# Zero products at TensorE's start made 16 bits and 512 columns wide, and an attention, feed-forward and experts kernel given a further order for its loads and first two blocks

## The chip, the cores and the metric

The kernel runs on one core of one Trainium2 chip. TensorE (PE) multiplies matrices into PSUM banks, VectorE (DVE), ScalarE (ACT) and GpSimd (POOL) do the elementwise work, and SyncE (SP) issues nearly all transfers. Each engine works through its own instructions in order and waits for the others by semaphores. The metric is device time in microseconds (us), the median of several executions.

## The reference

Three layers stand behind one another. The input has 2 sequences of 768 tokens with 8 heads of 64 columns, which makes 1536 tokens of 512 columns.

```python
# 1. attention with decay, in blocks of 64 (lam: one number a head)
intra = (q_b @ k_b.T * Dmask) @ v_b
inter = (q_b * lam_pow) @ kv_state
kv_state = lam**64 * kv_state + (k_b * rev_pow).T @ v_b
# 2. feed-forward, 512 -> 2048 -> 512
h = x @ w_in
g = where(h > 0, h, exp(min(h, 0)) - 1)
x = g @ w_out
# 3. one of 8 experts a token (and none where x @ w_skip <= 0)
y = gate * (relu(x @ w1[e]) @ w2[e])
out = x + y
```

The feed-forward weights come as 64-bit numbers and are made into 32-bit ones on the chip.

## The kernel before, in words

The tokens are worked on in chunks of 128 (12 of them, c = 0 to 11) and in blocks of three chunks. A product of 32-bit accuracy is made of three passes over a high and a low part (PASSES), so every weight and every activation is split in two.

**The prelude.** SyncE starts the loads in the order of LOADS: q and v are the two halves of an attention chunk (kq and kv in the traces), f a feed-forward weight. VectorE clears `zrow`, a table of zeros. TensorE then multiplies zeros by zeros (`warm`, L793 to L796, counts in WARM), with the two small products that build the decay tables (L801, L804) in between. Their results are never read. VectorE builds eight rows of the decay mask.

**The first two blocks.** Attention for chunks 0 to 5 and the first feed-forward steps are issued item by item from the table PLAN. An item is a name and its arguments, and the order of the table sets the order on every engine. A single step can only run when its own engine has come to it and its operands are there. The items that are spoken of below:

- MR:h, one mask row (VectorE, L810); LC, the table of powers lp (ScalarE)
- CV:f, B0:f, B1:f, B2:f, the conversion of weight f from 64 bits (ScalarE L161, VectorE L173, L176, L179); HI:f, its high part (ScalarE L184); LO:f and LP:f, its low part (L188, on VectorE and on GpSimd)
- S:c, the scores of chunk c (TensorE L248); M:c,half, their mask (VectorE L258); V:c, scores times values (TensorE L284)
- KD:c, keys times decay (GpSimd L275); KV:c, keys times values (TensorE L445); ST:c, their addition to the state (L468 for chunk 0 on ScalarE, else VectorE L472); DEC:c, the decay of the state (ScalarE L452)
- QD:c and QE:c, queries times powers (L269, on GpSimd and on VectorE); I:c, scaled queries times state (TensorE L284)
- XH:c, XL:c, the high and low part of the attention's result (L428, L432)
- F1:n, first feed-forward product (TensorE L497); R, X, E, GH, GL its activation in five steps on ScalarE and VectorE; F2:n, the second product (TensorE L544)

After the table (some 137 us into the span) loops with fixed orders take over: the rest of the feed-forward, with the attention of the second sequence between, the choice of experts, and the experts.

Of the kernel before, what the change touches and what calls it, by code (L numbers as in the profile page):

```python
# [10 lines left out]
BF16 = mybir.dt.bfloat16  # L11
# [5 lines left out]
P = 128  # L17
# [14 lines left out]
E = 8  # L32
# [2 lines left out]
XW = DM + 2  # L35
BIG = float(1 << 20)
PASSES = ((0, 0), (0, 1), (1, 0))
LOADS = "f0 q0 q1 v0 v1 q2 v2 q3 v3 f1 v4 q4 f2 q5 v5 f3 f4 f5 f6 f7 f8 f9"
PLAN = """
MR:5 MR:2 MR:0 MR:6 CV:0 S:0 MR:1 B0:0 MR:4 MR:7 B1:0 MR:3 KD:0 B2:0 KD:1 M:0,0 M:0,1 S:1 LC:0  # L40
KV:0 QD:1 ST:0 M:1,1 KD:2 HI:0 M:1,0 V:0 LO:0 XH:0 S:2 I:1 KV:1 M:2,1 QD:2 V:1 DEC:1 S:3 XH:1
ST:1 M:2,0 I:2 DEC:2 KV:2 QD:3 M:3,0 CV:1 KD:3 XL:0 V:2 M:3,1 V:3 ST:2 I:3 XL:1 KD:4 XH:2 XL:2
F1:0 B0:1 XH:3 B1:1 XL:3 B2:1 DEC:3 S:4 CV:2 M:4,1 KV:3 M:4,0 ST:3 R:0 HI:1 QD:4 X:0 E:0 S:5 V:4
I:4 M:5,0 M:5,1 LP:1 KV:4 GH:0 DEC:4 CV:3 GL:0 V:5 B0:2 QE:5 B1:2 F2:0 XH:4 ST:4 B2:2 I:5 XH:5
B0:3 XL:5 HI:2 F1:1 XL:4 F1:2 LP:2 R:1 X:1 E:1 GH:1 R:2 B1:3 X:2 GL:1 CV:4 B2:3 F1:3 F2:1 E:2
B0:4 F1:4 HI:3 GH:2 B1:4 GL:2 R:3 LO:3 X:3 R:4 E:3 X:4 F2:2 B2:4 GH:3 E:4 GL:3 F1:5 CV:5 F2:3
B0:5 HI:4 GH:4 LO:4 CV:6 B1:5 GL:4 B0:6 R:5 B2:5 F1:6 X:5 HI:5 R:6 E:5 B1:6 F2:4 X:6 GH:5 LO:5
F1:7 CV:7 E:6 GL:5 F1:8 GH:6 B2:6 R:7 B0:7 F2:5 X:7 E:7 B1:7 HI:6 GH:7 GL:7 GL:6 LO:6 R:8 X:8
CV:8 F2:6 E:8 GH:8 B2:7 B0:8 F1:9 B1:8 HI:7 GL:8 F1:10 F2:7 LO:7 B2:8 R:9 X:9 E:9 CV:9 B0:9 R:10
X:10 E:10 HI:8 F2:8 B1:9 GH:9 LO:8 B2:9 CV:10 B0:10 GL:9 B1:10 GH:10 HI:9 GL:10 F1:11 F1:12 R:11  # L50
LO:9 X:11 R:12 CV:11 E:11 X:12 F2:9 B2:10 B0:11 E:12 GH:11 F1:13 HI:10 GL:11 R:13 B1:11 B2:11
F2:10 GH:12 F2:11 GL:12 LO:10 F2:12 HI:11 CV:12 LO:11 CV:13 X:13 B0:12 B1:12 E:13 B0:13 F1:14
B2:12 F1:15 GH:13 R:14 X:14 E:14 GL:13 B1:13 GH:14 GL:14 F2:13 R:15 HI:12 LO:12 B2:13 X:15 CV:14
E:15 GH:15 B0:14 F1:16 GL:15 F2:14 B1:14 F2:15 R:16 X:16 E:16 HI:13 GH:16 F1:17 LO:13 CV:15
B2:14 GL:16 R:17 X:17 B0:15 HI:14 B1:15 F1:18 F2:16 E:17 GH:17 R:18 B2:15 X:18 GL:17 LO:14 F1:19
R:19 E:18 F2:17 F1:20 HI:15 GH:18 GL:18 X:19 E:19 F2:18 GH:19 R:20 F1:21 X:20 E:20 GH:20 LO:15
GL:19 F2:19 R:21 X:21 E:21 GL:20 F1:22 R:22 F2:20 GH:21 X:22 GL:21
"""


# [1 line left out]
def kernel(  # L62
# [11 lines left out]
    nc = tc.nc  # L74
# [18 lines left out]
    def bank(tag, bufs):  # L93
        return ps.tile([P, 512], F32, tag=tag, name=tag, bufs=bufs)
# [3 lines left out]
    def aux():  # L98
        return bank(aux_tag[0], 3)
# [9 lines left out]
    zrow = const.tile([P, P], F32, name="zrow")  # L109
# [375 lines left out]
    def where(n):  # L485
        return order[n] if n < 2 * NF else divmod(n, NF)
# [257 lines left out]
    if True:  # L744
# [12 lines left out]

        loads = LOADS.split()
        for item in loads[:3]:
# [19 lines left out]
            load(item)  # L779

        J = 2 * NF - TAIL1
        WARM = (4, 1, 5)
        manual = ExitStack()
        manual.enter_context(tc.manual_schedule())
        cv_gen = conv_ops(16)
# [6 lines left out]

        def warm(b, n):  # L793
            for i in range(n):
                nc.tensor.matmul(out=b[:, 0:P], lhsT=zrow[:, 0:P], rhs=zrow[:, 0:P],
                                 start=True, stop=True)  # L796

        idle_bank = bank("y", 3)
        warm(idle_bank, WARM[0])
        lamb, lpb = aux(), aux()  # L800
        nc.tensor.matmul(out=lamb[:, 0:H], lhsT=ones8, rhs=diag8, start=True, stop=True)  # L801
        warm(idle_bank, WARM[1])
        for k in range(4):
            nc.tensor.matmul(out=lpb[:, k * P:(k + 1) * P], lhsT=sel[:, k, :], rhs=powers,  # L804
                             start=True, stop=True)
        warm(idle_bank, WARM[2])
        nc.vector.tensor_copy(out=lam_b, in_=lamb[:, 0:H])

# [162 lines left out]
        for n in range(J, N - TAIL):  # L971
# [5 lines left out]
            b, f = where(n)  # L977
# [61 lines left out]
        for k in range(4):  # L1039
            nc.tensor.matmul(out=xg0[k // 2][:, k * P:(k + 1) * P],  # L1040
                             lhsT=early[:, k * P:(k + 1) * P], rhs=ident,
# [170 lines left out]
    with tc.If(over > 0):  # L1212
# [4 lines left out]
        for c in range(NCH):  # L1217
            nc.gpsimd.indirect_dma_start(
                out=slots[:, :], out_offset=bass.IndirectOffsetOnAxis(ap=idx[:, c:c + 1], axis=0),
                in_=gates[:, c, :], in_offset=None, bounds_check=E * NTOK - 1, oob_is_err=False)  # L1220
        for e in range(E):
# [3 lines left out]
            with tc.For_i(0, ne):  # L1225
                for k in range(8):
# [8 lines left out]
                    out=gt[:, :], out_offset=None, in_=slots[:, :],  # L1235
# [7 lines left out]
                    out=xg[:, :], out_offset=None, in_=out[:, :],  # L1243
# [73 lines left out]
```

## Time and profile before

| what | value |
|---|---|
| time, median of 3 runs | 437.74 us (437.14 to 438.39) |
| time of the profiled execution | 436.92 us |
| its span, first to last instruction | 434.8 us |
| TensorE busy | 97% of the span |
| VectorE busy | 74% of the span |
| GpSimd busy | 18% of the span |

The profiled execution lies 0.82 us under the median, and 2.1 us of it lie outside the span. TensorE's busy share is modelled, so that 97% says that it hardly waits, not that it runs at its peak.

### The profile page before, as it was taken

The numbers are of one execution on the slowest core, as the hardware profiler recorded it, in microseconds if no ns is written. First come the engines' busy times: TensorE is split into PE (matmuls) and PEld (weight loads), VectorE is DVE, ScalarE is ACT, GpSimd is POOL, SyncE is SP. The second block draws the span as 40 slices with busy tenths as digits, with TensorE's granted clock in tenths as the row PEclk, the third lists the DMA queues.
The fourth block names the chain that finished last, engine by engine and source line by source line (L and its number), as shares of the span: only waits on it lengthen the run. The fifth ranks groups of instructions, "written<-read, shape, count | busy, mean of one in ns | idle before, by whom it ended". The sixth has DMA issues, their size and how long they took to land.

```text
span 434.8 us, 8034 instructions
## 1 busy us (share of the span) xinstructions
PE 422.6 (97%) x3086; PEld 371.1 (85%) x3086; DVE 322.1 (74%) x703; ACT 239.0 (55%) x401; POOL 77.8 (18%) x107
## 2 busy tenths in 40 slices
PE   8999999999999999999999999999999999999992
PEld 8889999889998998998788998889897888888881
DVE  6898999998324447865887758776546799999960
ACT  2675787675443334533233445656526689888830
POOL 3853000001200120003141000222004202222211
PEclk9999999999999999999999999999999999999997
DMA  8999703998002131305141255336456899999301
GB/s 303 415 416 419 286 0 106 260 114 200 1 2 75 58 126 63 123 27 192 61 159 38 72 193 194 131 123 186 142 218 233 312 330 366 400 376 365 134 3 36
DMA packets 27649, 78.92 MB, mean 182 GB/s; under 512 B 4282, under 2 KB 8378, under 8 KB 25552
## 3 DMA queue, kind: packets, MB, share of 16 engines
q1 hardware_dynamic: 26000, 75.28, 51.1%
q0 software_dynamic: 1600, 3.03, 1.8%
q8 instruction: 26, 0.43, 0.4%
q14 instruction: 23, 0.19, 0.2%
HBM read 70.02 MB, written 10.51 MB: 185 GB/s over the span
## 4 chain that ended last, share of the span: by engine, by line
PE 82%; DVE 6%; issue 4%; DMA 3%; ACT 2%; POOL 1%; SPq 0%; POOLq 0%; ACTq 0%
PE h L497 29%; PE y L544 21%; PE h L1097 8%; PE aux L544 8%; PE y L1122 6%; PE aux L284 2%; DMA big<-in_wex_dram 1%; PE y L284 1%; DVE wa L139 1%; DMA big<-in_wff_dram 1%; PE aux L1108 1%; PE aux L599 1%; DMA out_dram<-o,ix 1%; PE aux L584 1%; PE aux L1077 1%
## 5 line engine op out<-in xcount | busy, mean ns | idle before, releaser
L497 PE MATMUL h<-xT,wa 128*128 128x384 f32 x480 | 89.8, 337 | 0.0
L497 PEld LDWEIGHTS h<-xT,wa 128*128 128x128 f32 x480 | 83.6, 188 | 3.0 <-issue 0.6
L544 PE MATMUL y<-wa,g 128*128 128x512 f32 x270 | 68.1, 396 | 0.0
L523 ACT ACTIVATE g<-e 128x384 fp32r<-128x384 f32 x64 | 33.5, 523 | 47.9 <-DVE e L517 47.9
L502 ACT ACTIVATE e<-h 128x384 f32<-128x384 f32 x64 | 31.0, 485 | 50.8 <-PE h L497 48.7
L544 PEld LDWEIGHTS y<-wa,g 128*128 128x128 f32 x270 | 49.6, 188 | 9.3 <-DVE g L528 0.3
L497 PE MATMUL h<-xT,wb 128*128 128x384 f32 x288 | 54.2, 336 | 0.0
L517 DVE SCALAR_TENSOR_TENSOR e<-e,h 128x384 f32<-128x384 f32 x64 | 35.1, 549 | 24.2 <-ACT e L505 23.9
L497 PEld LDWEIGHTS h<-xT,wb 128*128 128x128 f32 x288 | 50.5, 188 | 2.5 <-issue 0.5
L528 DVE TENSOR_TENSOR g<-e,g 128x384 fp32r<-128x384 f32 x64 | 36.2, 566 | 12.7 <-ACT g L523 12.7
L544 PE MATMUL y<-wb,g 128*128 128x512 f32 x162 | 40.6, 395 | 0.0
L628 DVE CUSTOM_DVE_ANT_0 zrow<-x,big 128x512 int8<-128x512 f32 x54 | 38.2, 707 | 0.6
L1097 PE MATMUL h<-wa,xgT 128*128 128x512 f32 x144 | 36.0, 397 | 0.1
L544 PEld LDWEIGHTS y<-wb,g 128*128 128x128 f32 x162 | 29.9, 188 | 5.5
L505 ACT ACTIVATE e<-e 128x384 f32<-128x384 f32 x64 | 33.5, 524 | 1.8
L139 DVE TENSOR_TENSOR wa<-big,wa 128x1024 fp32r<-128x1024 f32 x22 | 26.7, 1240 | 7.2 <-ACT wa L138 7.0
L1097 PEld LDWEIGHTS h<-wa,xgT 128*128 128x128 f32 x144 | 26.5, 188 | 5.7 <-ACT xgT L575 0.3
L727 POOL DMA_INDIRECT xe<-x,idx x12 | 12.2, 1015 | 98.2 <-DVE s L700 43.6
L343 POOL TENSOR_TENSOR big<-big,mask 128x512 f32<-128x512 f32 x6 | 7.3, 1214 | 106.6 <-DVE g L528 64.9
L138 ACT ACTIVATE wa<-big 128x1024 fp32r<-128x1024 f32 x22 | 22.4, 1057 | 3.9 <-DMA big<-in_wex_dram 3.9
L1122 PE MATMUL y<-wa,ht 128*128 128x512 f32 x96 | 23.7, 398 | 0.0
L139 DVE TENSOR_TENSOR wa<-ahead,wa 128x1024 fp32r<-128x1024 f32 x18 | 21.7, 1250 | 2.7 <-ACT wa L138 2.5
(231 smaller groups left out, 697.7 us busy)
## 6 DMA issues: line engine op xcount, KB each, us to landing
big<-in_wex_dram SPq DMA_DIRECT2D x17, 1024.0 KB, 6.1
ahead<-in_wex_dram SPq DMA_DIRECT2D x15, 1024.0 KB, 7.0
wb<-in_wff_dram SPq DMA_DIRECT2D x10, 1024.0 KB, 14.6
big<-in_wff_dram SPq DMA_DIRECT2D x6, 1024.0 KB, 8.9
big<-in_wgt_dram SPq DMA_DIRECT2D x18, 256.0 KB, 3.3
big<-in_kq_dram SPq DMA_DIRECT2D x6, 512.0 KB, 4.4
big<-in_kv_dram SPq DMA_DIRECT2D x6, 512.0 KB, 6.3
out_dram<-x SPq DMA_DIRECT2D x12, 256.0 KB, 2.6
```

The costliest lines, as they stand in the source:

```text
L138: nc.scalar.activation(out=w[:, 0, cs], in_=src, func=ACTF.Copy)
L139: nc.vector.tensor_tensor(out=w[:, 1, cs], in0=src, in1=w[:, 0, cs].bitcast(F32), op=ALU.subtract)
L497: nc.tensor.matmul(out=h, lhsT=w[:, wi, k * P:(k + 1) * P], rhs=xT[b][:, xi, k, :], start=(j == 0), stop=(j == 11))
L502: nc.scalar.activation(out=e, in_=h_t[n], func=ACTF.Relu, scale=-1.0)
L505: nc.scalar.activation(out=e_t[n], in_=e_t[n], func=ACTF.Exp, scale=-1.0)
L517: nc.vector.scalar_tensor_tensor(out=e, in0=e, scalar=-1.0, in1=h_t.pop(n), op0=ALU.add, op1=ALU.max)
L523: nc.scalar.activation(out=g[:, 0, :], in_=e, func=ACTF.Copy)
L528: nc.vector.tensor_tensor(out=g[:, 1, :], in0=e_t.pop(n), in1=g[:, 0, :].bitcast(F32), op=ALU.subtract)
L544: nc.tensor.matmul(out=y_t[b, t], lhsT=g[:, gi, t * P:(t + 1) * P], rhs=w[:, wi, 512:1024], start=(f == 0 and i == 0), stop=(f == NF - 1 a ...
L628: nc.vector.tensor_tensor_reduce(out=junk, in0=x2_t[c][:, 0:DM], in1=cols[0][:, slot * DM:(slot + 1) * DM], scale=1.0, scalar=0.0, op0=ALU ...
L1097: nc.tensor.matmul(out=h, lhsT=xgT_t[e][:, xi, k * P:(k + 1) * P], rhs=w_t[NF + 8 * e + k][:, wi, j * 512:(j + 1) * 512], start=(i == 0), ...
L1122: nc.tensor.matmul(out=y, lhsT=ht[:, hi, k, :], rhs=w_t[NF + 8 * e + 4 + k // 2][:, wi, (k % 2) * 512:(k % 2) * 512 + 512], start=(i == 0) ...
```

## The change

Three things change. The zero products read `zrow` as 16-bit numbers, and each fills a whole bank (512 columns in place of 128 columns of 32-bit numbers); their counts go from 4, 1 and 5 to 5, 2 and 5. In LOADS v0 now stands ahead of q1, and q4 ahead of v4. PLAN gets another order; most of it lies in the first two blocks, and further on single items move by a few places. In it QD:1 becomes QE:1 (from GpSimd to VectorE), LP:2 becomes LO:2 (the same way), and LO:14 becomes LP:14 (the other way).

```diff
-LOADS = "f0 q0 q1 v0 v1 q2 v2 q3 v3 f1 v4 q4 f2 q5 v5 f3 f4 f5 f6 f7 f8 f9"
+LOADS = "f0 q0 v0 q1 v1 q2 v2 q3 v3 f1 q4 v4 f2 q5 v5 f3 f4 f5 f6 f7 f8 f9"
 PLAN = """
-MR:5 MR:2 MR:0 MR:6 CV:0 S:0 MR:1 B0:0 MR:4 MR:7 B1:0 MR:3 KD:0 B2:0 KD:1 M:0,0 M:0,1 S:1 LC:0
+MR:2 CV:0 S:0 MR:6 MR:1 MR:0 MR:7 B0:0 MR:5 MR:4 MR:3 B1:0 M:0,0 KD:0 M:0,1 B2:0 S:1 LC:0 M:1,0
...
-        WARM = (4, 1, 5)
+        WARM = (5, 2, 5)
...
         def warm(b, n):
             for i in range(n):
-                nc.tensor.matmul(out=b[:, 0:P], lhsT=zrow[:, 0:P], rhs=zrow[:, 0:P],
+                nc.tensor.matmul(out=b, lhsT=zeros[:, 0:P],
+                                 rhs=zeros.rearrange("p (o n) -> p o n", o=1).to_broadcast([P, 2, 2 * P]),
                                  start=True, stop=True)
 
+        zeros = zrow.bitcast(BF16)
```

On VectorE, from the mask rows to the low part of the first weight, stood before (L810 mask rows, L173, L176 and L179 the bits of weight 0, L258 masks on scores, L188 the low part of weight 0):

```order
L810 SCALAR_TENSOR_TENSOR mask<-tab 128x128 x5
L173 TENSOR_SCALAR v<-v 128x1024
L810 SCALAR_TENSOR_TENSOR mask<-tab 128x128 x2
L176 SCALAR_TENSOR_TENSOR v<-big,v 128x1024
L810 SCALAR_TENSOR_TENSOR mask<-tab 128x128
L179 SCALAR_TENSOR_TENSOR v<-big,v 128x1024
L258 TENSOR_TENSOR pm_store<-h,mask 128x512 x2
L258 TENSOR_TENSOR pm_store<-y,mask 128x512 x2
L188 TENSOR_TENSOR wa<-v,wa 128x1024
```

On the same engine at the same place stands now (the mask rows are L812):

```order
L812 SCALAR_TENSOR_TENSOR mask<-tab 128x128 x5
L173 TENSOR_SCALAR v<-v 128x1024
L812 SCALAR_TENSOR_TENSOR mask<-tab 128x128 x3
L176 SCALAR_TENSOR_TENSOR v<-big,v 128x1024
L258 TENSOR_TENSOR pm_store<-h,mask 128x512 x2
L179 SCALAR_TENSOR_TENSOR v<-big,v 128x1024
L258 TENSOR_TENSOR pm_store<-y,mask 128x512
L269 TENSOR_TENSOR wb<-wb,lp 128x512
L258 TENSOR_TENSOR pm_store<-y,mask 128x512
L188 TENSOR_TENSOR wa<-v,wa 128x1024
```

The last mask row moved ahead of L176, both masks of chunk 0 moved ahead of L179, and the query scaling of chunk 1 (L269) stands between the masks of chunk 1.

On GpSimd the first products stood before as key scaling (L275) of chunks 0 and 1, query scaling (L269) of chunk 1, and so on with chunk 2:

```order
L275 TENSOR_TENSOR wb<-wb,mask 128x512 x2
L269 TENSOR_TENSOR wb<-wb,lp 128x512
L275 TENSOR_TENSOR wb<-wb,mask 128x512
L269 TENSOR_TENSOR wb<-wb,lp 128x512
L269 TENSOR_TENSOR wa<-wa,lp 128x512
```

On GpSimd at the same place stands now:

```order
L275 TENSOR_TENSOR wb<-wb,mask 128x512 x3
L269 TENSOR_TENSOR wb<-wb,lp 128x512
L269 TENSOR_TENSOR wa<-wa,lp 128x512
L275 TENSOR_TENSOR wa<-wa,mask 128x512 x2
L269 TENSOR_TENSOR wa<-wa,lp 128x512
```

The query scaling of chunk 1 is gone from it, so the three key scalings of chunks 0 to 2 follow one another. On TensorE the order of the items of the first two blocks is as before; only the zero products ahead of them differ.

## Rows read from the trace of the kernel before

**Rows 1.** The page: the span.

```profile
span 434.8 us, 8034 instructions
```

**Rows 2.** Busy time by stage; columns PE, PEld, DVE, ACT, POOL, granted clock, DMA.

```profile
12.00:35.00 23.00, 22.18 (x341) 19.73 (x341) 21.25 (x33) 15.24 (x31) 14.20 (x20) 1.00 1.02 415
35.00:137.00 102.00, 102.00 (x523) 92.76 (x519) 79.60 (x106) 64.55 (x104) 8.25 (x8) 1.00 0.56 143
```

**Rows 3.** Timeline of TensorE, the first 36 us: start us, us, instruction, idle before.

```profile
1.13 2.07 PE L795 MATMUL y<-zrow 128*128 128x128 f32 x8 [1.13 <-DVE zrow L761]
...
6.19 2.34 PE L795 MATMUL y<-zrow 128*128 128x128 f32 x10
8.46 1.79 PE L248 MATMUL h<-wb 64*128 64x128 f32 x16
10.09 1.06 PE L248 MATMUL y<-wb 64*128 64x128 f32 x16
12.18 0.69 PE L445 MATMUL aux<-wb 128*64 128x64 f32 x16 [1.03 <-POOL wb L275]
...
14.76 1.09 PE L284 MATMUL y<-wb,state 128*64 128x128 f32 x16
```

**Rows 4.** Timeline of SyncE's transfer issues, 5 to 18 us.

```profile
7.41 0.33 SPq L150 DMA_DIRECT2D big<-in_wff_dram  x1
8.70 0.33 SPq L232 DMA_DIRECT2D wa<-in_kv_dram  x1
...
12.54 0.33 SPq L229 DMA_DIRECT2D wa<-in_kq_dram  x1
```

**Rows 5.** Waits of SyncE, 5 to 18 us: total, times, longest.

```profile
SPq L232 <- DMA wb<-in_kq_dram: 0.9, 1, 0.9
```

**Rows 6.** Timeline of VectorE, 4 to 50 us.

```profile
7.30 0.69 DVE L173 TENSOR_SCALAR v<-v 128x1024 int32<-128x1024 int32 x1 [1.33 <-ACT v L161]
7.91 0.73 DVE L810 TENSOR_TENSOR_SCAN mask<-tab 128x128 f32<-128x128 f32 x2
8.55 1.20 DVE L176 SCALAR_TENSOR_TENSOR v<-big,v 128x1024 int32<-128x1024 int32 x1
...
11.12 1.28 DVE L258 TENSOR_TENSOR pm_store<-h,mask 128x512 f32<-128x512 f32 x2
12.32 1.28 DVE L258 TENSOR_TENSOR pm_store<-y,mask 128x512 f32<-128x512 f32 x2
14.87 1.60 DVE L188 TENSOR_TENSOR wa<-v,wa 128x1024 fp32r<-128x1024 f32 x1 [1.27 <-ACT wa L184]
...
26.17 1.28 DVE L258 TENSOR_TENSOR t<-aux,mask 128x512 f32<-128x512 f32 x2
...
31.41 0.68 DVE L269 TENSOR_TENSOR wa<-wa,lp 128x512 f32<-128x512 f32 x1
...
38.61 0.56 DVE L517 SCALAR_TENSOR_TENSOR e<-e,h 128x384 f32<-128x384 f32 x1 [1.34 <-ACT e L505]
...
45.11 1.22 DVE L188 TENSOR_TENSOR wa<-v,wa 128x1024 fp32r<-128x1024 f32 x1
```

**Rows 7.** Timeline of ScalarE, 12 to 15 us.

```profile
12.97 0.78 ACT L468 ACTIVATE state<-aux 64x256 f32<-64x256 f32 x2 [5.23 <-PE aux L445]
13.78 1.06 ACT L184 ACTIVATE wa<-v 128x1024 fp32r<-128x1024 f32 x1
```

**Rows 8.** Timeline of GpSimd, 9 to 14 us.

```profile
10.17 2.96 POOL L275 TENSOR_TENSOR wb<-wb,mask 128x512 f32<-128x512 f32 x2 [6.87 <-DVE mask L810]
```

**Rows 9.** The chain that ended last, 10 to 44 us: start us, us, what.

```profile
10.17 1.96 POOL wb L275
...
27.51 1.16 PE aux L248 x14
...
35.21 6.44 PE h L497 x36
41.65 2.06 PE y L544 x9
```

More of the change, by code (lines that the diff above doesn't have):

```diff
@@ L37 @@
 PASSES = ((0, 0), (0, 1), (1, 0))
-LOADS = "f0 q0 q1 v0 v1 q2 v2 q3 v3 f1 v4 q4 f2 q5 v5 f3 f4 f5 f6 f7 f8 f9"
+LOADS = "f0 q0 v0 q1 v1 q2 v2 q3 v3 f1 q4 v4 f2 q5 v5 f3 f4 f5 f6 f7 f8 f9"
 PLAN = """
-MR:5 MR:2 MR:0 MR:6 CV:0 S:0 MR:1 B0:0 MR:4 MR:7 B1:0 MR:3 KD:0 B2:0 KD:1 M:0,0 M:0,1 S:1 LC:0
-KV:0 QD:1 ST:0 M:1,1 KD:2 HI:0 M:1,0 V:0 LO:0 XH:0 S:2 I:1 KV:1 M:2,1 QD:2 V:1 DEC:1 S:3 XH:1
-ST:1 M:2,0 I:2 DEC:2 KV:2 QD:3 M:3,0 CV:1 KD:3 XL:0 V:2 M:3,1 V:3 ST:2 I:3 XL:1 KD:4 XH:2 XL:2
-F1:0 B0:1 XH:3 B1:1 XL:3 B2:1 DEC:3 S:4 CV:2 M:4,1 KV:3 M:4,0 ST:3 R:0 HI:1 QD:4 X:0 E:0 S:5 V:4
@@ L44 @@
[L44 to L55, printed above, removed]
@@ L56 @@
-R:19 E:18 F2:17 F1:20 HI:15 GH:18 GL:18 X:19 E:19 F2:18 GH:19 R:20 F1:21 X:20 E:20 GH:20 LO:15
-GL:19 F2:19 R:21 X:21 E:21 GL:20 F1:22 R:22 F2:20 GH:21 X:22 GL:21
+MR:2 CV:0 S:0 MR:6 MR:1 MR:0 MR:7 B0:0 MR:5 MR:4 MR:3 B1:0 M:0,0 KD:0 M:0,1 B2:0 S:1 LC:0 M:1,0
+KV:0 KD:1 QE:1 V:0 ST:0 M:1,1 KD:2 HI:0 LO:0 XH:0 S:2 I:1 KV:1 QD:2 DEC:1 ST:1 V:1 S:3 M:2,1
+M:2,0 XH:1 I:2 DEC:2 KV:2 V:2 QD:3 CV:1 M:3,1 M:3,0 XL:0 V:3 ST:2 I:3 XL:1 XH:2 B0:1 KD:3 XL:2
+B1:1 F1:0 DEC:3 XH:3 XL:3 B2:1 S:4 M:4,1 CV:2 KV:3 M:4,0 ST:3 R:0 B0:2 HI:1 KD:4 X:0 S:5 V:4
@@ new lines @@
+M:5,0 QD:4 I:4 E:0 M:5,1 LP:1 KV:4 GH:0 DEC:4 XH:4 CV:3 GL:0 V:5 B1:2 F2:0 QE:5 ST:4 B0:3 B2:2
+XL:4 I:5 XH:5 HI:2 XL:5 F1:1 R:1 LO:2 F1:2 X:1 R:2 E:1 GH:1 B1:3 X:2 GL:1 CV:4 B2:3 F1:3 F2:1
+E:2 B0:4 F1:4 HI:3 GH:2 B1:4 GL:2 R:3 LO:3 X:3 R:4 E:3 X:4 F2:2 B2:4 GH:3 E:4 CV:5 GL:3 F1:5
+F2:3 B0:5 HI:4 GH:4 LO:4 R:5 CV:6 B1:5 GL:4 B0:6 F1:6 X:5 B2:5 HI:5 E:5 R:6 B1:6 F2:4 X:6 GH:5
+LO:5 F1:7 CV:7 E:6 GL:5 F1:8 GH:6 B2:6 R:7 X:7 B0:7 F2:5 E:7 B1:7 HI:6 GH:7 GL:6 GL:7 LO:6 R:8
+X:8 CV:8 F2:6 E:8 GH:8 B2:7 B0:8 F1:9 B1:8 HI:7 GL:8 F1:10 F2:7 LO:7 B2:8 R:9 X:9 E:9 CV:9 B0:9
@@ new lines @@
+R:10 X:10 E:10 HI:8 F2:8 B1:9 GH:9 LO:8 F1:11 B2:9 CV:10 B0:10 GL:9 HI:9 GH:10 B1:10 GL:10 F1:12
+R:11 LO:9 X:11 E:11 R:12 X:12 F2:9 B2:10 CV:11 B0:11 E:12 GH:11 F1:13 HI:10 GL:11 B1:11 B2:11
+F2:10 GH:12 F2:11 R:13 GL:12 LO:10 F2:12 HI:11 CV:12 LO:11 CV:13 X:13 B0:12 B1:12 E:13 B0:13
+F1:14 B2:12 F1:15 R:14 X:14 E:14 GH:13 GL:13 B1:13 GH:14 GL:14 F2:13 R:15 HI:12 LO:12 B2:13 X:15
+CV:14 E:15 GH:15 B0:14 F1:16 GL:15 F2:14 B1:14 F2:15 R:16 X:16 E:16 HI:13 F1:17 LO:13 CV:15
+B2:14 GH:16 GL:16 R:17 X:17 HI:14 B0:15 B1:15 E:17 F1:18 R:18 B2:15 F2:16 X:18 GH:17 LP:14 GL:17
@@ L58 @@
+F1:19 R:19 E:18 F2:17 F1:20 HI:15 GH:18 GL:18 X:19 E:19 GH:19 R:20 F1:21 F2:18 X:20 E:20 GH:20
+LO:15 GL:19 R:21 GL:20 X:21 F1:22 E:21 GH:21 R:22 F2:19 F2:20 X:22 GL:21
 """
```

## The prediction

> **What bounds the kernel now.** I read the busy time by stage first. From 35 to 137 us TensorE is busy for 102.00 of 102.00 us, and in the stage before, 12 to 35 us, for 22.18 of 23.00 [rows 2]. So from 35 us on TensorE is the bound and nothing in the new order can make it shorter; a new order there can only add waits. What can be won is the time by which the dense part begins earlier. In the chain of waits that part shows as one long piece of TensorE from 35.21 us on [rows 9]. The end of the span (434.8 us [rows 1]) follows the start of that piece one to one, if nothing later gives way.
>
> Next I read who holds TensorE back before 35 us. Its timeline shows three places. The zero products and the two small ones run from 1.13 us, and the scores of chunk 0 (S:0) start at 8.46, right behind the last of them. S:0 is slow: 16 instructions take 1.79 us, and the same 16 for chunk 1 (S:1) take 1.06. Then TensorE stands idle for 1.03 us until GpSimd has scaled the keys of chunk 0 (KD:0), which lets KV:0 start at 12.18 [rows 3]. KD:0 itself had waited until 10.17 for the last mask row [rows 8]. The third place is 0.82 us of idle time between 12 and 35 us [rows 2]; in the chain it lies ahead of S:5, whose last 14 instructions start at 27.51 [rows 9], 0.06 us behind VectorE's masks of chunk 4 (26.17 plus 1.28 [rows 6]).
>
> That makes VectorE the engine to follow. From 7.30 us, when weight 0 has been copied, until 27.45 it works through a fixed list at the end of which TensorE waits. The one large wait inside this list is 1.27 us before LO:0 at 14.87, for ScalarE's high part of weight 0 [rows 6]. ScalarE came to that only at 13.78, because ST:0 stood ahead of it and waited for KV:0 [rows 7].
>
> The third thing to know is when the data land. SyncE issues a new load whenever an earlier one has landed. Its issues from 7.41 on are 1.28 us apart: 7.41, 8.70, two more, and 12.54 [rows 4]; the one at 8.70 waited for a q load [rows 5]. In the order of LOADS this gives landings of q0 7.40, q1 8.69, v0 9.96, v1 11.25 and q2 12.53.
>
> **The change part by part.** *Zero products.* Five of the old ones take 2.27 us (6.19 to 8.46 [rows 3]), 0.454 us each. No row shows the new form. The nearest is F2's product with 512 columns, nine in 2.06 us [rows 9], 0.229 us each, while TensorE runs at its upper clock. At half that clock it would be 0.458. So twelve new ones cost between 2.75 and 5.50 us, against 4.54 for the old ten. The granted clock reads 1.00 for the whole stretch, yet S:0 and S:1 differ as stated, so I take the durations: the zero products and most of S:0 ran at the lower level (1.2 GHz), and S:1 at the upper one (2.4 GHz), after 8.5 us of unbroken work. If the new form never brings the upper level earlier, S:0 starts some 0.5 us later, at 8.95 (the two products more; the first of them is partly hidden by the wait for the small product). If it brings the upper level before the last five, TensorE is free before q0 lands, and S:0 runs from 7.45 to 8.6. I take the second, since streaming with 512 columns is what the kernel does later, at the upper level throughout. S:0 then ends 1.5 us earlier, but nobody needs it then, as the next step shows.
>
> *Loads.* q1 and v0 swap: v0 lands at 8.69, q1 at 9.96. S:1 can now run from 10.0 to 11.1. q2 and later ones stay. KD:0 needs the last mask row and v0.
>
> *Mask rows and masks on VectorE.* The list starts at 7.30 as before, since f0 is still the first load. Three mask rows at some 0.36 us each (two in 0.73 [rows 6]) follow the first bit step at 7.91, and end at 9.05. KD:0 then starts at 9.1 in place of 10.17. Even with the 1.96 us that it took before [rows 9], it ends at 11.1, together with S:1. So KV:0 starts at 11.1 in place of 12.18, and TensorE's wait of 1.03 us is gone. Behind the mask rows come L176 (from 8.95, start to start 1.12 as before: 8.55 to the next at 9.67, of which nothing changes) until 10.1, then M:0,0 and M:0,1 until 11.3, then L179 until 12.45, M:1,0 until 13.0, QE:1 and M:1,1 until 14.2. All scores are there in time: S:0 by 8.6, S:1 by 11.1.
>
> *QE:1 for QD:1.* It costs VectorE 0.68 us (the same form at 31.41 [rows 6]). It frees GpSimd, which isn't a bound. I:1 needs it: it can start at 13.7, also behind S:2, which waits for q2 (12.53 plus 1.1).
>
> *LO:0.* ST:0 can run on ScalarE from 11.9 to 12.7 and HI:0 from there for 1.06 us [rows 7], to 13.8. VectorE comes to LO:0 at 14.2, so its wait of 1.27 us is gone.
>
> *Sum on VectorE up to the masks of chunk 4.* The same work in the list, minus 1.27 of waiting, plus 0.68 of QE:1, is a gain of 0.59 us. LO:0 took 1.60 us beside GpSimd's work and takes 1.22 elsewhere [rows 6], so up to 0.38 more comes back if GpSimd is quieter there; and some short waits behind it add up to 0.2. The bounds are 0.6 and 1.2; I take the middle, 0.9. TensorE's own limits allow it: its part from KV:0 on starts 1.08 us earlier, and it has 0.82 us of idle time to give.
>
> *From there to the dense part* TensorE works without a long gap, so F1:1 to F1:3 start 0.9 us earlier than at 35.21. B0:2 and B1:2 move ahead of the state's addition, within VectorE's list, at no cost that I can see: V:5 and I:5 then have their masks and state within 0.2 us of TensorE. LO:2 for LP:2 puts 1.22 us on VectorE where it stood idle for 1.34 us before E:1 at 38.61 [rows 6]. It costs nothing there; without that cover it would cost up to 1.2. From E:1 on VectorE's order is the old one for the next thirty rows. LP:14 takes 1.22 us off VectorE some 80 us later and puts it on GpSimd, which works for 8.25 of 102 us in that stage [rows 2].
>
> *Sum:* the profiled execution's 436.92 us minus 0.9 gives 436.0. Its time lies 0.82 us under the median of the runs shown (437.74), so carried to the median it is **436.84 us**, 0.2% faster.
>
> **The rivals.** *The wide products don't raise the clock.* S:0 runs from 8.95, and ends at 10.5 if the upper level comes when it came before. The first mask then starts at 10.5 in place of 10.1, and the gain shrinks by 0.4, to 0.5: 437.2. For it: ten old products in a row didn't raise it.
>
> *The gain is used up later.* VectorE and TensorE go side by side through the dense part, and a moved item there lets TensorE wait once. All 0.9 lost gives 437.7. Against it: VectorE was busy for 79.60 of 102 us there [rows 2].
>
> *Slower: the clock falls back.* TensorE now finishes S:0 at 8.6 and has nothing until q1 lands at 9.96, a gap of 1.4 us that wasn't there. If the clock falls to the lower level in it, and stays there through S:1, KV:0, V:0 and S:2, these take twice as long (S:1 alone is 1.06; KV:0 to S:2 go from 12.18 to 14.76, when I:1 starts, or 2.6 us [rows 3]). I:1 then starts at 10.0 plus twice 3.6, 17.2, where it started at 14.8, and with 0.8 us of idle time to take up, the end is 1.6 us later: 439.3. It decides only if the level stays low beyond S:1; before that q2's landing covers it. Against it: the wait of 1.03 us before KV:0 left the clock up.
> The Trainium skill, page "TensorE: Matmul & The Clock Gate", section "Why this matters for your kernels", says that gaps between bursts of products put the clock back to half rate. By that rule the price is that of this rival, if this gap is long enough. The trace of before shows one shorter gap without it.
>
> *More is won.* The three runs of before lie between 437.14 and 438.39, and the profiled one under all of them. If what differs between them is the moment at which the clock rises, then the wide products make every run a good one, and the gain is 0.9 plus most of 0.82: 436.0. Nothing in one trace can show that.
>
> **How the numbers follow.** Main case 0.46 (436.84, itself between 436.2 and 437.3), no earlier clock 0.17, used up later 0.13, clock falls 0.09, more is won 0.15. A measurement of this kernel tells some 0.3% (1.31 us) from no change, so faster begins below 436.43. That takes the case of more, and a third of the main one: 0.30. Slower is the falling clock, 0.09, since even a lost gain ends at 437.7. The rest is 0.61. The range goes from 435.4 (TensorE's 1.03 and 0.82 and half of S:0's slowness, all gained) to 438.2 (nothing gained, and a median as far off as the runs spread); it leaves out most of the falling clock.
>
> **What would show it.** Right: KV:0 near 11.1 us with no wait for KD:0, VectorE with no wait before LO:0, the second half of S:5 near 26.6, and the long piece of TensorE near 34.3. S:0 in 1.1 us shows that the clock is up; S:1 in 1.1 us shows that it stayed up. Wrong: S:1 of 2 us; TensorE waiting for VectorE between 40 and 137 us; or a dense part that starts where it did.

## The result, and the profile after

The changed kernel is slower: median 441.16 us (439.59 to 443.04, 6 runs) against 437.62 us (437.14 to 438.65, 6 runs) for the one before on the same chip, a ratio of 1.0078 with a 95% interval of 1.0056 to 1.0100. The forecast was 436.84 us, in a range up to 438.2. The profiled execution took 443.04 us, the longest of its six, and that of the kernel before 436.92, under all of its six: the two profiles lie 6.1 us apart where the medians lie 3.5 apart, so rows say where time is lost and medians how much.

The page of the changed kernel: span, busy time of the engines, and TensorE's granted clock in 40 slices.

```profile
span 441.0 us, 8021 instructions
...
PE 425.3 (96%) x3078; PEld 370.0 (84%) x3078; DVE 327.4 (74%) x704; ACT 239.0 (54%) x401; POOL 77.5 (18%) x106
...
PEclk9998999999999999999999999999999999999997
```

Its busy time by stage, with the columns of [rows 2]:

```profile
12.00:35.00 23.00, 20.14 (x298) 17.22 (x295) 22.70 (x31) 14.38 (x31) 13.95 (x18) 0.97 1.02 414
35.00:137.00 102.00, 102.00 (x518) 92.15 (x517) 82.90 (x107) 62.81 (x100) 7.86 (x8) 0.99 0.54 139
```

From 12 to 35 us TensorE was idle for 0.82 us before [rows 2]; now it is for 2.86. The clock, 1.00 before, is 0.97 there. So the loss sits ahead of the dense part, as the forecast gain should have. TensorE's timeline of the changed kernel says where:

```profile
7.57 1.16 PE L248 MATMUL h<-wb 64*128 64x128 f32 x16
9.95 1.16 PE L248 MATMUL y<-wb 64*128 64x128 f32 x16 [1.22 <-DMA wb<-in_kq_dram]
11.04 0.69 PE L445 MATMUL aux<-wb 128*64 128x64 f32 x16
...
26.72 1.65 PE L248 MATMUL aux<-wa 64*128 64x128 f32 x16 [0.47 <-DMA wa<-in_kq_dram]
...
31.81 0.69 PE L445 MATMUL aux<-wa 128*64 128x64 f32 x16 [1.54 <-DVE pm L258]
32.87 0.44 PE L284 MATMUL aux<-pm,wa 128*64 128x128 f32 x4 [0.38 <-DVE t L258]
...
34.07 3.72 PE L544 MATMUL y<-wa,g 128*128 128x512 f32 x9
...
38.74 6.62 PE L497 MATMUL h<-xT,wa 128*128 128x384 f32 x36
```

The first three rows are the forecast come true: S:0 and S:1 in 1.16 us each, KV:0 at 11.04 where it stood at 12.18 [rows 3]. At 31.81 it turns. KV:4 needs no mask as an operand, but it writes into a bank of `aux`, of which there are three: two hold the scores of chunk 5 and one the sums of chunk 4 (V:4 and I:4). So it waits until M:5,0 (`pm`, L258) has read the first, and that mask is 1.54 us late; the mask M:5,1, ahead of V:5, costs 0.38 more. Then F2:0's nine products take 3.72 us. The long piece begins at 38.74. TensorE's timeline of the kernel before has the same items at:

```profile
30.39 0.64 PE L445 MATMUL aux<-wa 128*64 128x64 f32 x16
...
31.83 2.35 PE L544 MATMUL y<-wa,g 128*128 128x512 f32 x9
...
35.14 6.51 PE L497 MATMUL h<-xT,wa 128*128 128x384 f32 x36
```

The piece began at 35.14 in this view (35.21 in the chain of [rows 9]), so it is 3.60 us late.

VectorE's timeline of the changed kernel shows what the mask stood behind:

```profile
12.86 0.95 DVE L269 TENSOR_TENSOR wb<-wb,lp 128x512 f32<-128x512 f32 x1
...
14.33 1.62 DVE L188 TENSOR_TENSOR wa<-v,wa 128x1024 fp32r<-128x1024 f32 x1
...
24.48 1.48 DVE L179 SCALAR_TENSOR_TENSOR v<-big,v 128x1024 int32<-128x1024 int32 x1
25.89 1.28 DVE L258 TENSOR_TENSOR t<-aux,mask 128x512 f32<-128x512 f32 x2
...
27.96 3.07 DVE L173 TENSOR_SCALAR v<-v 128x1024 int32<-128x1024 int32 x1
31.06 0.69 DVE L258 TENSOR_TENSOR pm<-aux,mask 128x512 f32<-128x512 f32 x1
```

The row of 27.96 is B0:2, one instruction of a form that takes 0.69 us [rows 6]. It took 3.07. And GpSimd's timeline shows what ran beside it:

```profile
8.98 1.95 POOL L275 TENSOR_TENSOR wb<-wb,mask 128x512 f32<-128x512 f32 x1 [5.68 <-DVE mask L812]
...
22.86 2.02 POOL L275 TENSOR_TENSOR wa<-wa,mask 128x512 f32<-128x512 f32 x1 [2.99 <-DMA wa<-in_kv_dram]
...
27.90 2.37 POOL L188 TENSOR_TENSOR wa<-v,wa 128x1024 fp32r<-128x1024 f32 x1 [0.80 <-ACT wa L184]
```

LP:1 started 0.06 us ahead of B0:2 and ended at 30.27. Add the 0.69 us that B0:2 takes by itself, and it ends at 30.96; it ended at 31.03. So it looks as if it did nothing until GpSimd's instruction was over. Below, such a wait inside an instruction's own row is called a hold.

In this execution the rest of the delay is the clock. The same stretch by microseconds, TensorE alone (busy, then granted clock):

```profile
33.00:34.00 1.00, 1.00 (x16) 0.83 0.96 385
34.00:35.00 1.00, 1.00 (x4) 0.50 0.94 393
...
36.00:37.00 1.00, 1.00 (x4) 0.50 1.02 426
37.00:38.00 1.00, 1.00 (x9) 0.97 1.00 418
```

TensorE had stood still before 31.81 and again before 32.87. From 33 to 34 us the clock fell, to 0.50, the lower level (1.2 GHz), and near 37 it came back. F2:0 lies in this stretch.

In the kernel before, B0:2 came only behind both masks of chunk 5 and GL:0, when GpSimd's LP:1 had ended (at 30.37). GpSimd's row there, and then VectorE's:

```profile
28.00 2.37 POOL L188 TENSOR_TENSOR wa<-v,wa 128x1024 fp32r<-128x1024 f32 x1 [0.60 <-ACT wa L184]
```

```profile
30.71 0.78 DVE L173 TENSOR_SCALAR v<-v 128x1024 int32<-128x1024 int32 x1
```

### The profile page after: what moved, and what is told of

Same layout as the page of the kernel before. It is cut to its first block, busy times and chain, and to the rows that moved or that the text cites. A ratio compares the mean times of both kernels' runs of the same rounds, so it can differ in the third digit from the quotient of the medians.

```text
span 441.0 us, 8021 instructions
## 1 busy us (share of the span) xinstructions
PE 425.3 (96%) x3078; PEld 370.0 (84%) x3078; DVE 327.4 (74%) x704; ACT 239.0 (54%) x401; POOL 77.5 (18%) x106
## 5 line engine op out<-in xcount | busy, mean ns | idle before, releaser
L544 PE MATMUL y<-wa,g 128*128 128x512 f32 x270 | 69.6, 403 | 0.0
L544 PEld LDWEIGHTS y<-wa,g 128*128 128x128 f32 x270 | 50.8, 192 | 9.7 <-ACT state L452 0.3
L628 DVE CUSTOM_DVE_ANT_0 zrow<-x,big 128x512 int8<-128x512 f32 x54 | 37.3, 690 | 0.6
L544 PE MATMUL aux<-wa,g 128*128 128x512 f32 x90 | 22.6, 396 | 0.0
```

What stands on the lines that cost most here:

```text
L544: nc.tensor.matmul(out=y_t[b, t], lhsT=g[:, gi, t * P:(t + 1) * P], rhs=w[:, wi, 512:1024], start=(f == 0 and i == 0), stop=(f == NF - 1 a ...
L628: nc.vector.tensor_tensor_reduce(out=junk, in0=x2_t[c][:, 0:DM], in1=cols[0][:, slot * DM:(slot + 1) * DM], scale=1.0, scalar=0.0, op0=ALU ...
```

## The experiments

Theory 1: VectorE's B0:2 and GpSimd's LP:1 exclude each other for whole instructions; the change put B0:2 where LP:1 runs; the masks behind it let TensorE wait, and the clock's fall is a consequence. Rivals: the zero products or the loads spoil the clock by themselves; or the new order costs in the dense part. In the table below "dense" is the start of TensorE's long piece in the one profiled execution. Each ratio is against executions of the kernel before on the same chip; the chips differ, so medians of different rows are not compared.

| kernel | what is in it | ratio to before (95%) | dense, us |
|---|---|---|---|
| before | | 1 | 35.14 |
| after | the change | 1.0078 (1.0056 to 1.0100) | 38.74 |
| e1_bits_back | after, B0:2 behind V:5 again | 1.0001 (0.9984 to 1.0018) | 34.99 |
| e2_low_on_vector | after, LP:1 as LO:1 on VectorE | 0.9995 (0.9977 to 1.0012) | 35.60 |
| e3_wide_alone | before, wide zero products | 1.0014 (0.9996 to 1.0033) | 36.61 |
| e4_bits_alone | before, B0:2 moved as in after | 1.0055 (1.0036 to 1.0074) | 37.42 |
| e5_clock_kept | after, TensorE kept busy in the wait | 1.0056 (1.0036 to 1.0075) | 37.24 |
| e6_narrow_back | e1, old zero products | 1.0004 (0.9991 to 1.0018) | 35.04 |
| e7_two_halves | after, LP:1 in two instructions | 1.0023 (1.0005 to 1.0040) | 36.01 |
| e8_back_filled | e1, zero products behind S:0 | 1.0002 (0.9988 to 1.0016) | 35.63 |
| e9_after_again | after, once more | one execution, 443.0 us | 38.79 |
| e10_q5_first | e1, q5 loaded ahead of f2 | 1.0045 (1.0025 to 1.0065) | 36.20 |
| e11_old_pair | e1, v4 loaded ahead of q4 | 1.0030 (1.0016 to 1.0043) | 35.75 |

**e1_bits_back** takes one item of the change back.

```diff
-... KV:3 M:4,0 ST:3 R:0 B0:2 HI:1 KD:4 ...
+... KV:3 M:4,0 ST:3 R:0 HI:1 KD:4 ...
-... CV:3 GL:0 V:5 B1:2 F2:0 ...
+... CV:3 GL:0 V:5 B0:2 B1:2 F2:0 ...
```

> The changed kernel with one item moved back: B0:2 (the one-input bit step of weight 2 on VectorE) stands behind GL:0 again, where GpSimd's subtract LP:1 is over. Theory 1 (VectorE's one-input step does not run while GpSimd's two-input subtract runs, TensorE stands idle behind it and its clock falls): the step takes 0.7 us in place of 3.07, KV:4 and V:5 lose their waits of 1.5 and 0.4 us, the granted clock stays 1.00, F2:0 takes 2.3 us in place of 3.7, and the whole is 437.0 to 437.6, at the time before or up to 0.15% under it (q5 lands at 26.7 us and holds S:5, so not the 0.9 us that were forecast). Theory 2 (the loss lies in the zero products, the loads or the rest of the order, and the long step only shows a late input): still 439 or more, with a long step elsewhere.

Median 439.01 us against 439.14, a ratio of 1.0001: the whole loss is gone. VectorE's timeline of e1, beside GpSimd's LP:1, which ran from 27.98 to 30.36:

```profile
28.21 0.69 DVE L258 TENSOR_TENSOR pm<-aux,mask 128x512 f32<-128x512 f32 x1 [0.27 <-PE aux L248]
28.82 0.54 DVE L517 SCALAR_TENSOR_TENSOR e<-e,h 128x384 f32<-128x384 f32 x1
29.28 0.68 DVE L258 TENSOR_TENSOR t<-aux,mask 128x512 f32<-128x512 f32 x1
29.95 0.82 DVE L528 TENSOR_TENSOR g<-e,g 128x384 fp32r<-128x384 f32 x1
30.69 0.79 DVE L173 TENSOR_SCALAR v<-v 128x1024 int32<-128x1024 int32 x1
```

Three operations that read one input from PSUM (`aux`, `h`) ran beside LP:1 at their usual length. Only GL:0, which reads two inputs from SBUF, was held, until LP:1's end: 0.82 us where it takes 0.56 with GpSimd quiet. So not every VectorE operation is held, and the ones that were moved behind B0:2 had been free. TensorE's timeline of e1:

```profile
30.11 0.64 PE L445 MATMUL aux<-wa 128*64 128x64 f32 x16
...
31.55 2.36 PE L544 MATMUL y<-wa,g 128*128 128x512 f32 x9
...
34.99 6.63 PE L497 MATMUL h<-xT,wa 128*128 128x384 f32 x36
```

Against these rows the changed kernel's KV:4 is 1.70 us late and F2:0 2.52; F2:0 takes 1.36 longer, and the dense part begins 3.75 later.

The Trainium skill, page "SBUF — State Buffer", section "SBUF: two separate sides", states a rule that gives the reason: VectorE and GpSimd share one pair of ports as an exclusive lock that the first to start keeps for its whole instruction, and on VectorE's side it concerns operations in a two-port mode, or with two SBUF inputs when GpSimd's operation reads SBUF. The page "VectorE: DVE Perf Modes", section "Mode 2×_2P — use both read ports for one tensor", puts a one-input operation on SBUF among the former. The traces agree on each: L173 (one input) takes 0.69 us for the columns on which L176 (two inputs) takes 1.20, both were held (3.07 here, 2.08 in e8 below), and the PSUM readers were not. The ports themselves show in no row; what the runs show is who waits for whom, and for how long.

**e2_low_on_vector** leaves B0:2 where the change put it and takes the other party away.

```diff
-... M:5,1 LP:1 KV:4 ... GL:0 V:5 B1:2
+... M:5,1 KV:4 ... GL:0 V:5 LO:1 B1:2
```

> The changed kernel with B0:2 left where it is, but the low part of weight 1 moved from GpSimd to VectorE (LP:1 becomes LO:1, behind GL:0), so that GpSimd does nothing beside B0:2. Theory 1: B0:2 takes 0.7 us at about 28 us, no wait at KV:4; VectorE has 1.2 us more to do ahead of the state's addition for chunk 4, so I:5 waits about 1 us: 437.8 to 438.8, slower than before by up to 0.25%. Theory 2: B0:2 still takes 3 us and the time stays at 441 or goes to 442.

B0:2 took 0.71 us (28.04), KV:4 did not wait (30.18), and the median is that of before (ratio 0.9995). So B0:2 in its new place costs nothing that can be measured when LP:1 is gone. GpSimd was not idle beside it: it ran its short fills, and the one that started at 28.16 took 0.64 us where it takes 0.13 in the changed kernel, so here it was the held one. It cost less than expected: VectorE's 1.22 us for LO:1 let I:5 wait 0.37 us, and nothing of it can be measured at the end.

**e4_bits_alone** is the reverse: the kernel before with this one item moved.

```diff
-... ST:3 R:0 HI:1 QD:4 ... GL:0 V:5 B0:2 QE:5 ...
+... ST:3 R:0 B0:2 HI:1 QD:4 ... GL:0 V:5 QE:5 ...
```

> The kernel before with one item moved: B0:2 right behind ST:3, as in the changed kernel; nothing else. Theory 1: the step starts at 28.2 us, 0.2 us behind LP:1 on GpSimd, and takes 2.8 to 3.1 us; M:5,0 and what follows is 2 to 2.4 us late, TensorE stands idle before KV:4, and if its clock falls F2:0 takes 3.7 us: 440 to 441.5, 0.5 to 0.9% slower. Theory 2: 0.7 us more on VectorE there, some of it hidden: 437.6 to 438.3.

It gave 0.55%, and its chain of waits runs through the held instruction:

```profile
28.21 3.06 DVE v L173
...
31.30 0.56 DVE e L517
31.85 0.61 DVE pm L258
...
32.51 0.69 PE aux L445 x16
```

KV:4 waited 1.98 us, the dense part began 2.28 us late, and 0.55% is 2.4 us (1.6 to 3.2). TensorE's clock stayed at 1.00 here.

**e7_two_halves** asks whether the hold lasts for an instruction or for as long as GpSimd has work.

```diff
-        eng = eng or nc.vector
+        if eng is not None and f == 1:
+            for cs in (slice(0, 512), slice(512, 1024)):
+                eng.tensor_tensor(out=w_t[f][:, 1, cs], in0=v_t[f][:, cs],
+                                  in1=w_t[f][:, 0, cs].bitcast(F32), op=ALU.subtract)
+            return
+        eng = eng or nc.vector
```

> The changed kernel with GpSimd's subtract LP:1 issued as two of 512 columns; everything else, the place of B0:2 too, as changed. If VectorE's one-input step is held for one GpSimd instruction at a time: it takes some 1.9 us (1.2 held and 0.7 of its own) in place of 3.07, the second half of LP:1 starts behind it, TensorE's wait before KV:4 shrinks from 1.5 to some 0.3 us, and the time is 1.2 to 2.6 us under the changed kernel's, 0.1 to 0.4% over the time before. If it is held until GpSimd has nothing left to do: 3.1 us again, and 0.8% over.

VectorE's row of B0:2 in e7:

```profile
28.12 1.72 DVE L173 TENSOR_SCALAR v<-v 128x1024 int32<-128x1024 int32 x1
```

and GpSimd's, both halves:

```profile
28.01 2.96 POOL L189 TENSOR_TENSOR wa<-v,wa 128x512 fp32r<-128x512 f32 x2 [0.75 <-ACT wa L184]
```

B0:2 slipped in between the halves. Its 1.72 us are about 1.0 us of the first half and its own 0.69, and now the second half waits for it: 2.96 us for both where one subtract takes 2.37. The loss shrank from 0.78% to 0.23%.

**e5_clock_kept** takes the clock's part away and leaves the hold: eight zero products stand in TensorE's list in the wait.

```diff
-M:5,0 QD:4 I:4 E:0 M:5,1 LP:1 KV:4 ...
+M:5,0 QD:4 I:4 W:8 E:0 M:5,1 LP:1 KV:4 ...
...
+            "W": lambda n: warm(bank("h", 2), n),
```

> The changed kernel with eight more zero products on TensorE between I:4 and KV:4, where it stands idle behind the held bit step (they need nothing that is late; their results are never read). The stall stays; only the clock can change. If the fall of the clock is a cost of its own: F2:0 takes 2.3 us in place of 3.7 in every run, the granted clock stays 1.00 from 30 to 40 us, and the time is 0.3 to 1.4 us under the changed kernel's, some 0.55% over the time before. If the clock falls from something else (the load of the chip, chance): F2:0 takes 3.7 us again, and the time stays at 0.8% over the time before.

B0:2 took 3.07 us as before, the clock stayed at 1.00, F2:0 took 2.34 us, and the dense part began 1.5 us earlier than in the changed kernel. So the profiles show the clock's part, 1.4 us at F2:0. The medians don't: 1.0056 and 1.0078 have intervals that overlap. The mean granted clock of whole executions says why. It is 0.991 in the profiled execution of the changed kernel and 0.990 in e9, where the fall is seen, and 0.994 or 0.995 in e4, e5 and e7, where there is none. Of the six executions of the changed kernel four have 0.994 or 0.995, so no such fall as far as the mean tells, and they took 440.66 to 442.50 us, as much as the median. That the clock adds to the median is not shown.

**e9_after_again** is the changed kernel itself.

> The changed kernel once more, unaltered, for a second profile. If the hold of B0:2 is a matter of the order, B0:2 takes 2.9 to 3.2 us again, KV:4 waits 1.3 to 1.7 us for M:5,0 and the dense part begins not before 37. The clock may fall at F2:0 or not: with it F2:0 takes 3.7 us and the dense part begins near 38.7, without it 2.35 us and near 37.3. If the slow pace of the dense part (nine products in 2.10 us) comes with this order, it shows again; if it belongs to one execution, nine products take 2.06 us.

B0:2 took 3.04 us, KV:4 waited 1.51, and the clock fell again, a little earlier: F2:0 took 3.18 us and the second half of V:5 was slow too. So in both profiles of this order the clock falls (by the mean clock not in most executions); in e4, with one wait of 1.98 us, and in e7 it does not.

**e3_wide_alone** and **e6_narrow_back** turn the zero products alone.

```diff
-        WARM = (4, 1, 5)
+        WARM = (5, 2, 5)
...
-                nc.tensor.matmul(out=b[:, 0:P], lhsT=zrow[:, 0:P], rhs=zrow[:, 0:P],
+                nc.tensor.matmul(out=b, lhsT=zeros[:, 0:P],
+                                 rhs=zeros.rearrange("p (o n) -> p o n", o=1).to_broadcast([P, 2, 2 * P]),
...
+        zeros = zrow.bitcast(BF16)
```

So it stands for e3, made from the kernel before; e6 is e1 with these lines turned back.

> The kernel before with the wide zero products and their counts 5, 2, 5 alone; order and loads as before. Theory 1: S:0 starts at 7.5 us at the upper clock, but VectorE's list is unchanged, so KV:0 still starts at 12.2 us and the time is that of before within 0.1%. Theory 2: the wide products cost the clock or the dense part's pace: 438.5 or more.

TensorE's timeline of e3:

```profile
7.51 1.16 PE L248 MATMUL h<-wb 64*128 64x128 f32 x16 [0.33 <-DMA wb<-in_kq_dram]
8.78 1.16 PE L248 MATMUL y<-wb 64*128 64x128 f32 x16
12.27 1.12 PE L445 MATMUL aux<-wb 128*64 128x64 f32 x16 [2.32 <-POOL wb L275]
13.18 1.92 PE L284 MATMUL aux<-pm_store,wb 128*64 128x128 f32 x16
```

The scores were done early, which nobody needs, and TensorE then waited 2.32 us for KD:0. Behind that wait KV:0 took 1.12 us and V:0 1.92, where they take 0.69 and 1.05 in the changed kernel; the granted clock is 0.50 from 13 to 15 us. TensorE's timeline of e4 has a wait of the same length at the same place, at a granted clock of 1.00:

```profile
12.29 0.69 PE L445 MATMUL aux<-wb 128*64 128x64 f32 x16 [2.30 <-POOL wb L275]
```

In e3 the dense part began at 36.61 in this profile; the median shows no difference that can be told.

> The changed kernel with B0:2 moved back behind GL:0 and the old zero products (32 bits, 128 columns, 4, 1 and 5 of them): what is left is the new order and the loads. Theory of the prediction (the wide products bring the upper clock earlier): S:0 starts at 8.0 or later, some or all of it at the lower clock, and VectorE's first mask up to 0.4 us later than with them; the whole 0 to 0.4 us slower than with the wide ones. Rival (the moment at which the clock rises is chance, whichever products run): no difference that can be measured, within 0.15% of the time before.

With the old products S:0 took 1.16 us from 7.49 in its profile, and the ratio is 1.0004. The old products can thus bring the upper level (2.4 GHz) as early as the new ones; in e4, which has them too, S:0 also took 1.16 us. So the slow S:0 of [rows 3] need not come from their width, and the wide ones vary as well: the last five took 1.24 us in the changed kernel and 1.72 in e5.

**e8_back_filled** fills the gap between S:0 and S:1 in e1.

```diff
-MR:2 CV:0 S:0 MR:6 ...
+MR:2 CV:0 S:0 W:4 MR:6 ...
...
+            "W": lambda n: warm(idle_bank, n),
```

> The changed kernel with B0:2 moved back behind GL:0, and four more zero products on TensorE behind S:0, where it stands idle for 1.1 us until q1 has landed. If falls of the clock in the first 12 us are part of what the runs differ by: the runs lie closer together and their median some 0.3 us under that with B0:2 moved back alone, 0.05 to 0.1% under the time before. If not: the time before within 0.1%.

The ratio is that of e1 (1.0002 against 1.0001), so this gap cost nothing that can be measured. Its profile shows how near the hold always is. VectorE's B1:1 in e8:

```profile
22.94 2.08 DVE L176 SCALAR_TENSOR_TENSOR v<-big,v 128x1024 int32<-128x1024 int32 x1
```

and GpSimd's KD:4:

```profile
22.88 1.06 POOL L275 TENSOR_TENSOR wa<-wa,mask 128x512 f32<-128x512 f32 x1 [2.87 <-DMA wa<-in_kv_dram]
```

In the changed kernel L176 started first (22.75), and KD:4, 0.11 us later, was the one held (2.02 us). Here KD:4 was 0.06 us ahead, and VectorE, on which TensorE waits, lost 0.86 us.

**e10_q5_first** and **e11_old_pair** ask where the rest of the forecast gain went, with the hold of B0:2 away. S:5's second half waits for q5 in the changed kernel (the row of 26.72), and KD:4 comes later than before since v4 does.

```diff
-LOADS = "f0 q0 v0 q1 v1 q2 v2 q3 v3 f1 q4 v4 f2 q5 v5 f3 ..."
+LOADS = "f0 q0 v0 q1 v1 q2 v2 q3 v3 f1 q4 v4 q5 f2 v5 f3 ..."  (e10)
+LOADS = "f0 q0 v0 q1 v1 q2 v2 q3 v3 f1 v4 q4 f2 q5 v5 f3 ..."  (e11)
```

> The changed order with B0:2 back behind V:5, and q5 loaded ahead of f2. If the rest of the forecast gain was lost at the landing of q5 (S:5's second half waited 0.54 us for it), that wait is gone, S:5's second half runs near 26.3 in place of 26.80, and the dense part begins 0.3 to 0.6 us before 34.99, at 34.4 to 34.7; the ratio is 0.9985 to 1.0000. If the masks of chunk 4 on VectorE (to 27.17 us) set the start, the dense part begins at 34.9 to 35.1, and f2's later landing shows as a later B0:2 only.

S:5's second half came at 26.69, now behind VectorE's mask of chunk 4: 0.11 us won. The masks set the start, not q5. And f2's later landing cost more than I expected: CV:2 stands ahead of R:0 on ScalarE and took it along to 27.70, so LP:1 started at 29.18, and GL:0, a two-input operation, ran into it:

```profile
29.55 0.56 DVE L517 SCALAR_TENSOR_TENSOR e<-e,h 128x384 f32<-128x384 f32 x1 [0.58 <-ACT e L505]
...
30.70 1.28 DVE L528 TENSOR_TENSOR g<-e,g 128x384 fp32r<-128x384 f32 x1
```

The state's addition was late, I:5 waited 0.81 us for it, and the ratio is 1.0045.

> The changed order with B0:2 back, and v4 ahead of q4 as before. If v4's later landing holds B2:1 (0.27 us) by way of KD:4, KD:4 starts near 21.6 in place of 22.88 and runs against L176 or not at all, B2:1 takes 1.22 us, and the masks of chunk 4 end 0.2 to 0.3 us earlier, at 26.9; the dense part moves by no more than that, and the ratio stays within 0.998 to 1.002. If KD:4 meets L176 instead, VectorE loses as much there and nothing changes.

Both my cases missed. KD:4 met L173, which neither names. B2:1 took 1.21 us, as expected, but the masks of chunk 4 ended at 28.07 and not at 26.9. GpSimd's KD:4 in e11:

```profile
21.62 1.06 POOL L275 TENSOR_TENSOR wa<-wa,mask 128x512 f32<-128x512 f32 x1 [1.66 <-DMA wa<-in_kv_dram]
```

and VectorE's B0:1:

```profile
21.77 1.46 DVE L173 TENSOR_SCALAR v<-v 128x1024 int32<-128x1024 int32 x1 [0.21 <-ACT v L161]
```

The hold of 0.77 us put off a part of the attention's result, F1:0 waited 0.56 us for it, and the kernel is 0.3% slower. In this order the swap of q4 and v4 is worth keeping, for a reason that the forecast did not have.

No version beat both kernels: e1, e2, e6 and e8 can't be told from the one before (all intervals within 0.25%).

## Why the prediction was wrong

**The step that failed** is "B0:2 and B1:2 move ahead of the state's addition, within VectorE's list, at no cost that I can see". That sentence misread the order: ST:3 stands ahead of both steps in both kernels, and in the kernel before B0:2 (30.71) and B1:2 (32.01) already ran ahead of ST:4 (33.15). What B0:2 passed is M:5,0, E:0, M:5,1 and GL:0, and so it came to stand beside LP:1. The forecast put this at nothing and did not ask what GpSimd does in that moment. Its masks, said to be within 0.2 us of TensorE, came 1.54 and 0.38 us late. The hold is 2.38 us (3.07 minus 0.69). e1 and e2 show that without it, by either party, the kernel equals the one before, and e4 that by itself it makes 0.55%. The other 0.2% lies within the intervals; in the profiled execution the clock's fall behind the wait comes on top (1.4 us at F2:0), and what it adds to the median is not shown (e5).

**The trace of before had the pattern**, and I read it as a loose "beside GpSimd's work": LO:0 at 1.60 us [rows 6] and two key scalings in 2.96 [rows 8], where a low part takes 1.22 elsewhere [rows 6] and one key scaling 1.06 (the row of e8). KD:0 of the changed kernel is the plainest: started at 8.98 while L176 ran until 10.01, it ended at 10.93, 0.92 us after it, little less than a quiet one takes in all (1.06). The KD:0 of before was the same: started at 10.17 while L179 ran from 10.01 to 11.21, it ended at 12.13, also 0.92 us after it.

**Right:** KD:0 and KV:0 1.1 us earlier (forecast 11.1, came 11.04; partly luck, since the 1.96 us that I took for KD:0 held a hold, and the new place brought another of the same length); no wait before LO:0 (forecast 14.2, came 14.33); S:0 at the upper level from 7.57; S:1 in 1.16 us behind a wait of 1.22, so the clock did not fall there. Right in the main is that the end follows the start of the dense part: 2.28 us in the profile for 2.4 in the runs of e4, 0.87 for 1.0 in e7. It is no exact rule: in e3, e10 and e11 the two differ by 0.7 to 0.9 us, and a profile is one execution.

**Mis-sized:** the gain of 0.9 us up to the masks of chunk 4. They ended at 27.17 instead of 27.45, a gain of 0.28. Three rows of this list were held: QE:1 took 0.95 us and not 0.68 (KD:1 ran beside it), LO:0 1.62 where I let half of its excess of 0.38 come back, 1.41 (KD:2), B2:1 1.48 and not 1.22 (KD:4); together 0.74 us, more than the 0.62 that are missing. In e1, where B0:2 is not held beside LP:1, 0.15 us of this is left at 34.99, and the median shows none of it. e10 rules out that the landing of q5 took the rest.

**The rivals:** the falling clock has the sign of the result, but not its cause or place: the clock stayed up between S:0 and S:1, and in the profiled execution it fell at 33.6 us, behind a wait that the hold made. It fell behind waits of 1.54 and 0.38 us there and of 2.32 in e3, and not behind 2.30 and 1.98 in e4, so the length of a wait alone doesn't decide here. By the Trainium skill, page "TensorE: Matmul & The Clock Gate", section "Why this matters for your kernels", long enough gaps between bursts of products put the clock back to half rate; that alone does not tell these waits apart.

"More is won" had half a point. Beside e1 to e4, 11 of the 35 executions of before have a mean granted clock of at most 0.991 and a median of 439.71 us, the other 24 one of 438.87; the profile of e3 (0.990) shows such a fall behind the wait before KV:0. But the wide products don't end it: with them alone (e3) 4 of 12 executions have at most 0.991. The new order does, with old products (e6) as with wide ones: in e1, e2, e6 and e8, where KV:0 follows S:1 without a wait, it is none of 48. Even so their medians are that of before, and those of e6 and e8 (438.48 and 438.67) lie above the 437.79 of the executions of before over 0.991 beside them. So the new order seems to cost some tenths elsewhere; where, no run shows. That LO:2 for LP:2 costs nothing, and what LP:14 does, was tried only within e1, where the sum of all is nothing.

**Open:** in the profiles of the changed kernel and e5 nine products of the dense part follow each other in 2.10 us between 45 and 95 us, in that of before in 2.06, and in e9, the same kernel as the changed one, in 2.08, all at a granted clock of 1.00. It makes some 1.1 us in the first profile. It isn't the order alone, since two executions of one kernel differ; what it is I can't say. The profile of before is also the shortest of all from the start of the dense part on, 399.7 us where the others have 401.0 to 402.5, e1 with its equal median 401.4. Why the clock falls behind the waits of the changed kernel and e3 and not behind those of e4 is open as well.

## What to carry to other kernels

Before an elementwise step is moved on VectorE, look up what GpSimd runs at that time: if both work in SBUF (VectorE with two inputs there, or with one in the quick form, like B0's 0.69 us for 1024 columns), the later one waited for the other's whole instruction in these runs, and a 0.7 us step cost 3. Price the items that it is moved past, since they are what arrives late, and put the operations that read PSUM beside GpSimd's long ones. A row that takes longer than its form elsewhere may be a hold: lay its start and end beside the other engine's before taking it for a rate.

## What the runs showed that I had not expected

The hold goes either way by who starts first, even by 0.06 us (e8), so that the same order on these two engines can lose 0.9 us on VectorE or on GpSimd. It is for whole instructions: cutting GpSimd's subtract in two cut the hold from 2.38 to 1.03 us (e7). Whether TensorE has the upper level at S:0 varied with the old zero products (1.79 us in [rows 3], 1.16 in e4 and e6). And it is the order, not the products, that goes with the end of the executions of 0.991 and less, without a gain in the median.
